# Four tiles instead of two for the decoded words of layer 2's weights, and the plain block's weight sums four steps later

## The chip, the cores and the metric

The kernel runs on one core of a Trainium2 chip. The metric is device time in microseconds (us) for one execution; times are given as the median of several runs. The five engines are TensorE (PE; its weight loads appear as PEld), VectorE (DVE), ScalarE (ACT), GpSimd (POOL) and SyncE (SP). SP issues nearly all DMA transfers here, from one queue that is worked through in order.

## What is computed

Three layers over 6016 tokens (2 batches of 3008) of 256 channels, all in float32 with weights that arrive as 64-bit words:

```python
def _attn_ref(x, filt_r, filt_i):            # a convolution by FFT along the sequence
    Y = np.fft.rfft(x, axis=1) * (filt_r + 1j * filt_i)[None, :, :]
    return np.fft.irfft(Y, n=x.shape[1], axis=1)
def _moe_ref(x, w_gate, w_val, w_out):       # layer 1: 256 -> 1536 -> 256
    g = x @ w_gate
    return (g * (1.0 / (1.0 + np.exp(-g))) * (x @ w_val) @ w_out)
def _moe2_ref(x, w_in, w_out):               # layer 2: 256 -> 2048 -> 256
    h = x @ w_in
    return h * np.clip(h + 3.0, 0.0, 6.0) / 6.0 @ w_out
```

## The kernel before

**Stages.** First comes the FFT stage (matrix products with small cosine and sine matrices), to about 70 us. Then come the six token blocks of layer 1, and after them the six blocks of layer 2. Layer 1's block 0 is the **plain block**; it is cut into two halves of 512 tokens. Blocks 1 to 5 of layer 1 and all blocks of layer 2 are computed in **units**.

**Precision.** Every operand of a product is split into a high and a low part (ACT copies to the high part, DVE or POOL subtracts it to get the low one), and three of the four partial products are summed.

**The plain block** is the loop `for t in range(2 * plain)` at L560, 24 steps t. A step computes gate and value of one chunk f of 128 hidden channels for one half (`l1`, L229), ACT applies Silu (L586), DVE multiplies (L593); in every odd step the hidden values of two chunks are split (L607) and the output products of the step pair before run (`l2_plain`, L237). Beside it the layer 1 weights are decoded, one chunk f at a time, from 64-bit to 32-bit words. The list comprehension at L588 sets when: `lead` (ACT `start`, L183, then DVE parts 0 to 2: L192, L194, L197) at t = 2f-6, `rest` (DVE L200, L202, L119) at t = 2f-5, and `part` (ACT L395 writes the high part into `wall(f)`, POOL the low part, SP stores the words into `w1f[f]`, L400) at t = 2f-4. Chunk f is first used at step 4*(f//2) + f%2, so chunks 10 and 11 in steps 20 and 21.

**Weight sums.** The units use a seven-product scheme for 2x2 blocks of matrices and need four sums of weight quarters for each chunk (`weight_sums`, L241, four POOL operations). For chunks 0 to 4 this happens in the plain block, L616 to L627: SP reloads the words from `w1f[q]` (L523, tile `y`), two steps later POOL forms the sums, one step later SP stores them (L520). Steps 19 to 21 ask for the first three units' weights (`ask_unit`, SP, L497, tile `st`), steps 20 and 22 split them (`split_unit`, L501: three ACT casts at L509, five POOL subtractions, tiles `wu` and `wo`). In steps 19 and 20 `to_time` (L156) brings the next block's tokens from the FFT stage into PSUM.

**A unit s** (loop at L829) takes 21 matmuls of `product` (L654) in seven threes and 12 output matmuls (L699) of the unit before it, in three fours. Unit s also splits the weights of unit s+2 and asks for those of unit s+4. The spots "N", "A", "B", "T", "C" inside a unit run jobs that other code has hung there. Blocks 1 to 5 start at units 0, 12, 24, 36 and 48.

**Decoding layer 2's weights** hangs on blocks 2 to 5, 12 units each: four halves per block, 16 in all. A half loads 512 raw words (`ask_w2`, SP, L178, tile `raw`), ACT takes absolute values into tile `wa` (L183), DVE makes tile `ww` and works back into `wa` (L192, L194, L197, L200, L202), POOL adds the two (L119 through `finish_w2`, L805), and every second half POOL forms sums into tile `sm`. One unit later SP stores `ww` into `w2f[g]` (L800) and `sm` (L802). The pool `late` gives each of `raw`, `wa` and `ww` two tiles, `sm` has one. In the fourth unit of a block (units 15, 27, 39, 51) spot "B" holds, in this order, the POOL adds of the second half, DVE's L192 and L194 of the third half, and ACT's L183 of the fourth half:

```python
free_spots = [(u, name) for u in range(7) for name in "ABC" if (u, name) not in ((0, "B"), (1, "A"))]
...
    places = [(s + u, name) for u, name in free_spots[4 * q:4 * q + 5]]
    add(u - 2, "N", ask_w2, g, i)
    add(u - 1, "B", lambda g, i: dec2[g, i].start(), g, i)
    spread(places, [(decode_w2, g, i, 0, 1), (decode_w2, g, i, 2), (decode_w2, g, i, 3), (decode_w2, g, i, 4), (finish_w2, g, i)])
```

In the same unit, behind the L119 `gv` sum, PE's third group of two products ends in DVE's L119 `h<-gv,h` (the value `v1`), which reads the PSUM bank that PE's next product (S4) adds to.

Of the kernel before, what the change touches and what calls it, by code (L numbers as in the profile page):

```python
# [9 lines left out]
F32 = mybir.dt.float32  # L10
# [6 lines left out]
P = 128  # L17
# [6 lines left out]
F1, F2 = DFF1 // P, DFF2 // P  # L24
# [54 lines left out]
def fft_conv_glu_mlp(ctx: ExitStack, tc: tile.TileContext, x, filt, mats, sgn, w1, w2, out):  # L79
# [19 lines left out]
    def wall(f):  # L99
        return wall_a[:, f] if f < 8 else wall_b[:, f - 8]  # L100
# [10 lines left out]
    def bank(tag="gv"):  # L111
        turn[tag] += 1
        return banks[tag][(turn[tag] - 1) % 4]
# [4 lines left out]
    def plus(out, a, b, engine=None):  # L118
        (engine or nc.vector).tensor_tensor(out=out, in0=a, in1=b, op=ALU.add)  # L119
# [28 lines left out]
    def to_time(g, first, n, accs, a, at=0):  # L148

        t0, t1 = turns(first, n)  # L150
        lo, hi = 32 * first, 32 * first + n // 2
        for t in range(t0, t1):
            i0, i1 = max(lo, t * N1), min(hi, (t + 1) * N1)
            for o in range(0, P, 64):
                for r in range(2):
                    nc.tensor.matmul(accs[r][o:o + 64, at + i0 - lo:at + i1 - lo],  # L156
                                     g[rows(r, N1P), t - t0, o:o + 64],
                                     mat[rows(r, N1P), FIN + i0 - t * N1:FIN + i1 - t * N1])
# [7 lines left out]
    class Decode:  # L166
# [17 lines left out]

        def part(self, i, engine=None):
            if self.w is None:
                self.w = self.pool.tile([P, self.n], F32, tag="ww", name="ww")
            v, a, w = nc.vector, self.a, self.w
            au, wu, low, high = a.bitcast(U32), w.bitcast(U32), self.raw[:, :, 0], self.raw[:, :, 1]

            if i == 0:
                v.tensor_scalar(out=a, in0=a, scalar1=LEAST, scalar2=MOST, op0=ALU.max, op1=ALU.min)  # L192
            elif i == 1:
                v.tensor_scalar(out=wu, in0=au, scalar1=3, scalar2=0x3FFFFFF8,  # L194
                                op0=ALU.logical_shift_left, op1=ALU.bitwise_and)
            elif i == 2:
                v.scalar_tensor_tensor(out=wu, in0=high, scalar=0xC0000000, in1=wu,  # L197
                                       op0=ALU.bitwise_and, op1=ALU.bitwise_or)
            elif i == 3:
                v.tensor_scalar(out=au, in0=wu, scalar1=0xFF800000, scalar2=None, op0=ALU.bitwise_and)  # L200
            elif i == 4:
                v.scalar_tensor_tensor(out=a, in0=low, scalar=2.0 ** -52, in1=a, op0=ALU.mult, op1=ALU.mult)  # L202
            else:
                plus(w, w, a, engine or nc.gpsimd)
# [16 lines left out]
    def half(k):  # L221
        return blocks[k][2] * N2 // 2

    def l1(acc, w, c, xs, part=(0, 1, 2)):

        for i in part:
            r, v = ((0, 0), (0, 1), (1, 0))[i]
            for k in range(2):
                nc.tensor.matmul(acc, w[:, r, c[k]:c[k] + P], xs[:, v, k],  # L229
                                 start=(r, v, k) == (0, 0, 0), stop=(r, k) == (1, 1))  # L230

    def l2_plain(k, p, hs, first, last):
        for v, ws in ((0, (1, 0)), (1, (0,))):
            for j in range(2):
                for i in range(2):
                    for r in ws:
                        yield lambda v=v, j=j, i=i, r=r: nc.tensor.matmul(  # L237
                            banks["a"][2 * j + k], wall(2 * p + i)[:, r, (1 + j) * P:(2 + j) * P], hs[:, v, i],
                            start=first and (v, i, r) == (0, 0, 1), stop=last and (v, i) == (1, 1))
# [8 lines left out]
    def new_hs():  # L248
        return mlp.tile([P, 4096], F32R, tag="hs", name="hs")

    def new_h():
        return mlp.tile([P, 2048], F32, tag="h", name="h")
# [10 lines left out]
    with tc.manual_schedule():  # L263
# [130 lines left out]
        def high_w1(f):  # L394
            nc.scalar.copy(out=wall(f)[:, 0], in_=dec[f].w)  # L395
# [44 lines left out]
        def form(j):  # L440
            if j == 0:
                xsd["both"] = new_xs()
            xsd[j] = xsd["both"][:, j * 2048:(j + 1) * 2048].rearrange("p (v k n) -> p v k n", v=2, k=2)
            accs = [bank("a"), bank("a")]
            for a in range(2):
                to_time(gt[j][a], FIRST[j][0], 512, accs, a, 256 * a)
            return accs

        def form_end(j, acc):
            for r in range(2):  # L450
                split(*time_halves(xsd[j], acc, r))
# [108 lines left out]
        for t in range(2 * plain):  # L560
            p, i = divmod(t, 2)
            k, g_ = steps[p]
            f = 2 * g_ + i
            if t == 2 * plain - 5:
                scope.close()
                lower.close()
                for name in ("stage", "raw"):
                    pool[name] = ctx.enter_context(tc.tile_pool(name=name, bufs=1))

            if i == 0:  # L570
                hid[p] = new_h().rearrange("p (a n) -> p a n", n=512)
            gate, val = bank(), bank()
            for part in ((0, 1), (2,)):
                l1(gate, wall(f), (3 * P, 4 * P), xsd[k], part)
                l1(val, wall(f), (0, 5 * P), xsd[k], part)
            if t == 0:
                acc1 = form(1)
            if t in (19, 20):
                turned_x = [bank(), bank()]
                to_time(g1[t - 19], *blocks[1][1:2], 2 * half(1), turned_x, t - 19)  # L580
            if i == 1 and p >= 1:
                kq, gq = steps[p - 1]
                for step in l2_plain(kq, gq, hid.pop(p - 1), gq == 0, gq == G1 - 1):
                    step()
            h = hid[p][:, i]
            nc.scalar.activation(out=h, in_=gate, func=AF.Silu)  # L586

            lead, rest, part = ([f_ for f_ in range(2, F1) if t == 2 * f_ + d] for d in (-6, -5, -4))  # L588
            for f_ in part:
                high_w1(f_)  # L590
            for f_ in lead:
                dec[f_].start()
            nc.vector.tensor_tensor(out=h, in0=h, in1=val, op=ALU.mult)  # L593
            if t == 0:
                form_end(1, acc1)
            for f_ in part:
                low_w1(f_, nc.gpsimd)
                if f_ + 2 < F1:
                    load_dec(f_ + 2)
            for f_ in rest:  # L600
                dec[f_].rest(nc.vector)
            for f_ in lead:
                dec[f_].part(0)
                dec[f_].part(1)
            if i == 1:
                hs = new_hs()[:, :2048].rearrange("p (v a n) -> p v a n", v=2, a=2)
                split(hs[:, 0], hs[:, 1], hid[p][:, 0:2])  # L607
                hid[p] = hs
            for f_ in lead:
                dec[f_].part(2)  # L610
            if t in (8, 10, 12, 14):
                store(1, 1, t - 8)
                store(1, 1, t - 7)
            if t == 9:
                g1 = load_g(*blocks[1][:2], 2 * half(1))
            if 6 < t < 19:  # L616
                q, r = divmod(t - 7, 2)
                if r == 0:
                    if q == 0:
                        spare = new_y()  # L620
                        wq = load_wq(0, spare[:, :768])
                    else:
                        sums(q - 1, wq, spare[:, 1536:].rearrange("p (s c) -> p s c", c=P), nc.gpsimd)
                        if q < 5:
                            wq = load_wq(q, spare[:, 768 * (q % 2):768 * (q % 2) + 768])
                elif q > 0:
                    keep_sums(q - 1)  # L627
            if t in (19, 20, 21):
                ask_unit(t - 19)
            if t in (20, 22):  # L630
                split_unit((t - 20) // 2)
            if t in (19, 20):
                if t == 19:
                    xr[1] = new_raw()
                    begin_x(1)
                evacuate(1, turned_x, t - 19)
            if t > 19:
                for i in ((0,), (1, 2), (3,), ())[t - 20]:
                    differ(1, i)
                for i in ((0, 3), (5, 4, 1), (2, 6), ())[t - 20]:  # L640
                    x_high(1, i)
                for i in ((0,), (3, 5), (4, 1), (2, 6))[t - 20]:
                    x_low(1, i)
# [172 lines left out]
        for k in range(2, n_block):  # L816
            s = F1 * (k - 1)
            for q in range(4):
                g, i = divmod(4 * (k - 2) + q, 2)
                places = [(s + u, name) for u, name in free_spots[4 * q:4 * q + 5]]  # L820
                u, name = places[0]
# [145 lines left out]
```

## Time and profile before

| | |
|---|---|
| median of 3 runs | 1200.11 us (1197.69 to 1200.96) |
| the profiled execution | 1203.46 us, its span 1201.7 us |
| PE busy | 1130.1 us, 94% of the span |
| DVE busy | 852.8 us, 71% |
| ACT busy | 752.6 us, 63% |
| POOL busy | 595.3 us, 50% |
| mean granted TensorE clock | 0.967 of full speed |

A busy share is a mean over stages. Busy time on PE includes time at the lower clock (1.2 instead of 2.4 GHz), where the same matmul takes twice as long. In the rows below, an arrow names what ended an idle time; "x4" counts instructions merged into one row.

### The profile page before, as it was taken

The page shows a single profiled execution, that of the slowest core. Times are in us where ns is not written, and L with a number is a line of the kernel's source. Part 1 is how long each engine was busy: PE and PEld are TensorE (multiplying, and loading weights), DVE is VectorE, ACT ScalarE, POOL GpSimd, SP SyncE. Part 2 cuts the span into 40 slices and gives each one's busy share as a digit, 9 for nine tenths or more (in the row PEclk, how much of TensorE's full clock was granted, in tenths as well). Part 3 has the DMA queues.
Part 4 walks back from the last instruction along what each step waited for, and adds up shares of the span by engine and source line. Part 5 has one row for each costly group of instructions (what it writes and reads, how often), then busy time and mean ns, then how long its engine had stood idle before and what let it go on. Part 6 is the DMA issues. An engine that isn't in the chain of part 4 may idle for free. (4 is left out here: it accounts for less than half of the span.)

```text
span 1201.7 us, 19167 instructions
## 1 busy us (share of the span) xinstructions
PE 1130.1 (94%) x7232; PEld 934.0 (78%) x7232; DVE 852.8 (71%) x1164; ACT 752.6 (63%) x1363; POOL 595.3 (50%) x779
## 2 busy tenths in 40 slices
PE   9989999999599869968996999999999999999998
PEld 7768878888488748846885888888888888888887
DVE  4979966678378756846784887767767767677665
ACT  4644437677267636744773777777777677777664
POOL 4733446746375635555454764544544445335440
PEclk9989989999799979988997999999999999999999
DMA  9965943732633352362324333232232322322300
GB/s 304 282 179 178 281 149 108 201 125 95 172 98 105 127 127 84 106 160 98 108 99 171 108 133 105 73 139 73 73 143 73 124 89 73 140 73 73 108 25 33
DMA packets 59484, 150.65 MB, mean 125 GB/s; under 512 B 5536, under 2 KB 27424, under 8 KB 57888
## 3 DMA queue, kind: packets, MB, share of 16 engines
q1 hardware_dynamic: 58848, 148.92, 38.7%
q8 instruction: 56, 0.92, 0.3%
q10 hardware_dynamic: 544, 0.52, 0.1%
q14 instruction: 36, 0.29, 0.1%
HBM read 117.17 MB, written 32.24 MB: 124 GB/s over the span
## 5 line engine op out<-in xcount | busy, mean ns | idle before, releaser
L654 PE MATMUL gv<-xs,wu 128*128 128x512 f32 (+1 forms) x2268 | 577.6, 391 | 56.6 <-DVE h L119 55.8
L116 POOL TENSOR_TENSOR wu<-st,wu 128x224 fp32r<-128x224 f32 x432 | 308.3, 744 | 489.4 <-ACT wu L509 476.4
L654 PEld LDWEIGHTS gv<-xs,wu 128*128 128x128 f32 x2268 | 427.5, 190 | 145.0 <-DVE h L119 59.3
L699 PE MATMUL a<-hs,wo 128*128 128x512 f32 (+1 forms) x1872 | 479.9, 387 | 0.0
L699 PEld LDWEIGHTS a<-hs,wo 128*128 128x128 f32 x1872 | 353.2, 189 | 67.5 <-ACT hs L687 0.3
L687 ACT CAST hs<-h 128x512 fp32r<-128x512 f32 (+3 forms) x216 | 172.6, 799 | 176.5 <-DVE h L681 101.3
L116 DVE TENSOR_TENSOR hs<-h,hs 128x1024 fp32r<-128x1024 f32 (+3 forms) x228 | 233.6, 1025 | 65.9 <-ACT hs L687 60.5
L116 POOL TENSOR_TENSOR wo<-st,wo 128x256 fp32r<-128x256 f32 x156 | 147.7, 959 | 0.0
L683 DVE SCALAR_TENSOR_TENSOR h<-h,gv 128x512 f32<-128x512 f32 (+1 forms) x144 | 96.4, 670 | 23.3 <-ACT h L677 23.0
L509 ACT CAST wu<-st 128x384 fp32r<-128x384 f32 x216 | 110.6, 563 | 0.0
L119 DVE TENSOR_TENSOR gv<-gv,h 128x512 f32<-128x512 f32 (+1 forms) x108 | 74.0, 685 | 50.7 <-PE gv L654 45.1
L675 ACT ACTIVATE h<-gv 128x512 f32<-128x512 f32 (+1 forms) x120 | 70.5, 588 | 59.3 <-PE gv L654 58.9
L677 ACT ACTIVATE h<-gv 128x512 f32<-128x512 f32 (+1 forms) x144 | 84.0, 583 | 16.3 <-PE gv L654 16.2
L119 DVE TENSOR_TENSOR h<-gv,h 128x512 f32<-128x512 f32 (+1 forms) x108 | 72.9, 675 | 24.5 <-PE gv L654 24.4
L862 ACT COPY gv<-gv 128x512 f32<-128x512 f32 (+1 forms) x108 | 60.8, 563 | 45.4 <-PE gv L654 41.8
L683 DVE SCALAR_TENSOR_TENSOR h<-h,h 128x512 f32<-128x512 f32 (+1 forms) x48 | 32.7, 681 | 59.6 <-ACT h L677 59.6
L866 ACT COPY h<-gv 128x512 f32<-128x512 f32 (+1 forms) x108 | 62.4, 578 | 18.7 <-PE gv L654 17.9
L681 DVE TENSOR_TENSOR h<-h 128x512 f32<-128x512 f32 (+1 forms) x60 | 60.1, 1001 | 3.5 <-ACT h L675 3.2
L116 DVE TENSOR_TENSOR xs<-raw,xs 128x512 fp32r<-128x512 f32 (+1 forms) x77 | 56.8, 739 | 0.1
L509 ACT CAST wo<-st 128x256 fp32r<-128x256 f32 (+1 forms) x108 | 54.2, 501 | 0.0
L194 DVE TENSOR_SCALAR ww<-wa 128x512 uint32<-128x512 uint32 x16 | 9.5, 593 | 60.7 <-DMA w2f<-ww 59.9
L552 ACT CAST xs<-raw 128x512 fp32r<-128x512 f32 (+1 forms) x77 | 45.7, 608 | 3.0 <-DVE raw L116 3.0
(88 smaller groups left out, 940.2 us busy)
## 6 DMA issues: line engine op xcount, KB each, us to landing
st<-w1f SPq DMA_DIRECT2D x60, 576.0 KB, 4.1
st<-w2f SPq DMA_DIRECT2D x48, 704.0 KB, 4.0
raw<-w_in SPq DMA_DIRECT2D x16, 512.0 KB, 4.4
ring<-x_in SPq DMA_DIRECT2D x30, 256.0 KB, 5.4
x<-w_in SPq DMA_DIRECT2D x9, 768.0 KB, 5.5
d<-turned SPq DMA_DIRECT2D x32, 192.0 KB, 5.5
w1f<-x SPq DMA_DIRECT2D x12, 384.0 KB, 2.7
yd<-y SPq DMA_DIRECT2D x4, 1024.0 KB, 6.4
```

The costliest lines, as they stand in the source:

```text
L116: (engine or nc.vector).tensor_tensor(out=out, in0=a, in1=b, op=ALU.subtract)
L119: (engine or nc.vector).tensor_tensor(out=out, in0=a, in1=b, op=ALU.add)
L509: nc.scalar.copy(out=to[:, 0, at:at + hi - lo], in_=src[:, lo:hi])
L654: nc.tensor.matmul(acc[:, :n], w[:, r, FORM[a] * P:(FORM[a] + 1) * P], xs_part(k, v, i), start=start and q == 0, stop=q == 2, skip_group_c ...
L675: nc.scalar.activation(out=self.value(t, 0), in_=src, func=AF.Silu)
L677: nc.scalar.activation(out=self.value(t, a), in_=src, func=AF.Relu, bias=3.0)
L681: nc.vector.tensor_tensor(out=self.value(t, 0), in0=self.value(t, 0), in1=src, op=ALU.mult)
L683: nc.vector.scalar_tensor_tensor(out=self.value(t, a), in0=self.value(t, a), scalar=6.0, in1=src, op0=ALU.min, op1=ALU.mult)
L687: nc.scalar.copy(out=self.hs[:, t, :, 0, :self.n], in_=self.value(t))
L699: yield lambda t=t, v=v, a=a, j=j, r=r: nc.tensor.matmul(banks["a"][2 * j + t][:, :n], self.wo[:, r, (2 * a + j) * P:(2 * a + j + 1) * P], ...
L862: nc.scalar.copy(out=b2[:, :n], in_=b1[:, :n])
L866: nc.scalar.copy(out=u.s7, in_=b3[:, :n])
```

## The change

The tag `ww` gets four tiles where the pool's default of two held before. In the plain block, `lead`, `rest` and `part` of chunks 10 and 11 come one step later (`+ (f > 9)`), and the chain that loads, sums and stores the weight sums of chunks 0 to 4 comes four steps later (q counts from step 11, not 7). No instruction is added or removed.

```diff
@@ Decode.part @@
             if self.w is None:
-                self.w = self.pool.tile([P, self.n], F32, tag="ww", name="ww")
+                self.w = self.pool.tile([P, self.n], F32, tag="ww", name="ww", bufs=4)
@@ the plain block @@
-            lead, rest, part = ([f_ for f_ in range(2, F1) if t == 2 * f_ + d] for d in (-6, -5, -4))
+            lead, rest, part = ([f_ for f_ in range(2, F1) if t == 2 * f_ + d + (f_ > 9)] for d in (-6, -5, -4))
...
-            if 6 < t < 19:
-                q, r = divmod(t - 7, 2)
+            if 10 < t < 23:
+                q, r = divmod(t - 11, 2)
```

**On DVE, in unit 15** (names: `wa`, `ww` and `raw` are the decode tiles, `gv` a PSUM bank, the brackets hold the semaphores waited for, DMAHW those of DMA transfers):

```order
 L192 TENSOR_SCALAR wa<-wa 128x512 [waits Pool_49]
-L194 TENSOR_SCALAR ww<-wa 128x512 [waits DMAHW0_49,DVE_49]
+L194 TENSOR_SCALAR ww<-wa 128x512 [waits DVE_49]
 L119 TENSOR_TENSOR h<-gv_110,h 128x480 [waits PE_49]
 L681 TENSOR_TENSOR h<-h,gv_109 128x480 [waits PE_49,Activation_49]
-L197 SCALAR_TENSOR_TENSOR ww<-raw,ww 128x512 [waits DVE_49]
+L197 SCALAR_TENSOR_TENSOR ww<-raw,ww 128x512 [waits DMAHW0_49,DVE_49]
```

The order stays; L194 no longer waits for a DMA transfer, and the wait that L197 shows now is for the transfer that brings `raw`.

**On DVE, in steps 17 to 19 of the plain block** (`x_122` holds the chunk that is decoded, here chunk 11; `gv_109` and `gv_107` are the values of an even and an odd step):

```order
 L197 SCALAR_TENSOR_TENSOR x_122<-x_122 128x768
-L593 TENSOR_TENSOR h<-h,gv_109 128x512
+L593 TENSOR_TENSOR h<-h,gv_107 128x512
 L200 TENSOR_SCALAR x_122<-x_122 128x768
 L202 SCALAR_TENSOR_TENSOR x_122<-x_122 128x768
 L119 TENSOR_TENSOR x_122<-x_122 128x768
-L116 TENSOR_TENSOR hs<-h,hs 128x1024
-L593 TENSOR_TENSOR h<-h,gv_109 128x512
 L593 TENSOR_TENSOR h<-h,gv_107 128x512
 L116 TENSOR_TENSOR hs<-h,hs 128x1024
```

In step 18 the multiplication (L593, `gv_109`) and before it the low part of step 17's hidden values (L116 `hs`) stood behind the three operations that finish chunk 11; now those two stand ahead of the three, and step 19's multiplication (`gv_107`) comes behind them.

**On POOL, at the end of the plain block** (`wall_b` is the low part of a decoded chunk of layer 1, the `y` rows are one chunk's sums, `wu` and `wo` a unit's split):

```order
 L116 TENSOR_TENSOR wall_b<-x_122,wall_b 128x768
-L116 TENSOR_TENSOR wu<-st,wu 128x224 x4
-L116 TENSOR_TENSOR wo<-st,wo 128x256
+L119 TENSOR_TENSOR y<-y 128x128
+L116 TENSOR_TENSOR y<-y 128x128 x3
+L116 TENSOR_TENSOR wu<-st,wu 128x224 x4
+L116 TENSOR_TENSOR wo<-st,wo 128x256
+L119 TENSOR_TENSOR y<-y 128x128
+L116 TENSOR_TENSOR y<-y 128x128 x3
```

and on SP, whose queue runs in this order:

```order
 L523 DMA y<-w1f_91 128x768
-L400 DMA w1f_97<-x_122 128x768
+L497 DMA st<-w1f_87 128x1152
 L520 DMA w1f_90<-y 128x512
-L400 DMA w1f_98<-x_122 128x768
+L497 DMA st<-w1f_88 128x1152
+L497 DMA st<-w1f_89 128x1152
 L520 DMA w1f_91<-y 128x512
```

The sums of chunk 3 now stand ahead of unit 0's split on POOL and those of chunk 4 ahead of unit 1's; on SP the store of chunk 3's sums stands between the requests for units 0 and 1, and that of chunk 4's behind the request for unit 2.

## Rows read from the trace of the kernel before

**Rows 1.** The page, part 2: PE's busy tenths and clock in 40 slices.

```profile
PE   9989999999599869968996999999999999999998
PEclk9989989999799979988997999999999999999999
```

**Rows 2.** Waits, whole span: waiter, releaser: total us, times, longest.

```profile
DVE ww L194 <- DMA w2f<-ww: 59.9, 4, 16.8
...
PE gv L654 <- DVE h L119: 55.8, 4, 15.8
...
ACT wa L183 <- POOL ww L119: 15.9, 4, 4.2
...
PE gv L156 <- DVE h L593: 2.1, 1, 2.1
```

**Rows 3.** Timeline, units 14 to 16: start us, length us, engine, line [idle before].

```profile
301.50 2.14 PE L654 MATMUL gv<-xs,wu 128*128 128x480 f32 x9
...
306.95 2.53 POOL L116 TENSOR_TENSOR wu<-st,wu 128x224 fp32r<-128x224 f32 x4 [3.04 <-issue]
...
307.82 1.03 PE L699 MATMUL a<-hs,wo 128*128 128x480 f32 x4
...
311.56 0.67 ACT L183 ACTIVATE wa<-raw 128x512 f32<-128x512 f32 x1 [3.91 <-POOL ww L119]
...
322.77 0.43 DVE L194 TENSOR_SCALAR ww<-wa 128x512 uint32<-128x512 uint32 x1 [15.93 <-DMA w2f<-ww]
...
323.82 3.97 PE L654 MATMUL gv<-xs,wu 128*128 128x480 f32 x9 [14.97 <-DVE h L119]
324.35 0.59 ACT L687 CAST hs<-h 128x480 fp32r<-128x480 f32 x1 [12.13 <-DVE h L681]
...
327.58 1.28 PE L699 MATMUL a<-hs,wo 128*128 128x480 f32 x4
```

**Rows 4.** DMA issues at 306.00 and 309.76 us: last number us to landing.

```profile
st<-w1f SPq DMA_DIRECT2D x1, 576.0 KB, 8.9
...
w2f<-ww SPq DMA_DIRECT2D x1, 256.0 KB, 12.9
```

**Rows 5.** Window of 1 us: busy PE, PEld, DVE, ACT, POOL, then PE's clock.

```profile
311.00:312.00 1.00, 0.00 (x0) 0.00 (x0) 0.00 (x0) 0.44 (x1) 0.92 (x2) 0.52 0.98 403
```

**Rows 6.** POOL by form, 286 to 307 us: count, busy us, mean ns.

```profile
L116 POOL TENSOR_TENSOR wu<-st,wu 128x224 fp32r<-128x224 f32 x12 | 9.5, 821 | 7.2 <-ACT wu L509 4.1 <-issue 3.0
L116 POOL TENSOR_TENSOR wo<-st,wo 128x256 fp32r<-128x256 f32 x3 | 3.5, 1151 | 0.0
L119 POOL TENSOR_TENSOR ww<-ww,wa 128x256 f32<-128x256 f32 x2 | 2.0, 1040 | 0.0
```

**Rows 7.** Timeline, PE and DVE in the plain block, steps 12 to 22.

```profile
126.81 5.60 PE L229 MATMUL gv<-xs,wall_a 128*128 128x512 f32 x24
...
134.97 5.60 PE L229 MATMUL gv<-xs,wall_a 128*128 128x512 f32 x24
...
152.57 3.80 PE L229 MATMUL gv<-xs,wall_b 128*128 128x512 f32 x16
...
160.96 2.79 PE L156 MATMUL gv<-mat,g 48*64 48x5 f32 x94 [2.10 <-DVE h L593]
...
171.23 1.60 PE L156 MATMUL gv<-mat,g 48*64 48x5 f32 x96
...
178.34 5.60 PE L229 MATMUL gv<-xs,wall_b 128*128 128x512 f32 x24
```

**Rows 8.** Windows of 1 us in step 19, columns as in rows 5.

```profile
161.00:162.00 1.00, 1.00 (x40) 1.00 (x43) 0.50 (x1) 0.46 (x1) 0.98 (x1) 0.50 1.05 287
...
167.00:168.00 1.00, 1.00 (x5) 0.77 (x4) 0.00 (x0) 0.00 (x0) 0.00 (x0) 0.66 1.00 399
```

**Rows 9.** DVE by form, 102 to 134 us.

```profile
L200 DVE TENSOR_SCALAR x<-x 128x768 uint32<-128x768 uint32 x4 | 2.3, 575 | 0.0
```

**Rows 10.** DVE by form, 134 to 162 us.

```profile
L200 DVE TENSOR_SCALAR x<-x 128x768 uint32<-128x768 uint32 x3 | 2.9, 962 | 0.0
```

## The prediction

> **What bounds the kernel now.** I read the page's slices first: PE is busy nearly everywhere, except in single slices between 300 and 660 us, where its clock falls too [rows 1]. So PE sets the time, and what can be won lies in those holes. The list of waits names them: DVE's L194, which writes `ww`, waits four times for the DMA store of an older `ww`, 59.9 us in all, and PE's L654 waits four times for DVE's L119, 55.8 us in all [rows 2]. Four is once per block 2 to 5. The timeline of unit 15 joins the two: PE stops when its output products end at 307.82 + 1.03 = 308.85 us, DVE resumes with L194 at 322.77 us after 15.93 us of waiting, and PE follows at 323.82 us [rows 3]. L194 stands ahead of the L119 that reads PE's PSUM bank, so a decode step that nobody needs yet holds back the product. The store is late because it was issued at 309.76 us, behind large transfers in SP's queue, and took 12.9 us to land [rows 4].
>
> The hole also costs clock: with PE stopped since 308.85 us, the granted clock from 311 to 312 us is 0.52 [rows 5], the lower level of 1.2 GHz. After the restart nine matmuls take 3.97 us where they took 2.14, and the next four 1.28 instead of 1.03 [rows 3], which is 1.83 + 0.25 = 2.1 us more per hole. Together the four holes cost 55.8 + 4 x 2.1 = 64.2 us.
>
> **The four tiles.** With four tiles a decode half writes a `ww` that was last used a whole block before. The wait of L194 goes, 64.2 us with its clock. What is late next stands in the same unit: ACT's L183 needs the `wa` tile of the half before, which POOL's L119 sets free; `wa` keeps its two tiles. It waits four times today, 15.9 us in all [rows 2], under cover of the longer hole, so it costs nothing; with the cover gone, it is exposed. Behind L183 on ACT stands L687, which writes the high part that PE's output products of the next unit read first.
>
> How long that wait becomes: POOL starts unit 15's split at 306.95 us [rows 3] and does four `wu`, one `wo` and two `ww` operations before `wa` is free. With DVE at work beside it those take 0.821, 1.151 and 1.040 us each [rows 6], so 3.28 + 1.15 + 2.08 = 6.5 us, until 313.5. With DVE waiting, POOL let ACT go at 311.56 us [rows 3]. DVE will be busy for the first half of this time and then wait for ACT itself, so I take the middle, 312.5. Then L183 (0.67) and L687 (0.59) [rows 3] make the high part ready at 313.8; by the ends at 312.8 and 314.7. PE, no longer held, runs its nine products in 2.1 us from 308.85 and would want it at 310.95. It waits 2.85 us (1.9 to 3.8). In step 19 of the plain block an idle time of only 2.1 us [rows 7] was followed by a clock of 0.50 [rows 8]. So I add the 2.1 us of lower clock to a wait of 2.85 us, and leave them out at the short end of 1.9 us, for which no row shows a fall. Per block that is 4.95 us, for four blocks 20 us (7.6 to 23.6). The gain from the four tiles is 64.2 - 20 = 44 us (40.6 to 56.6).
>
> The other waits nearby keep a cover. The next stage load lands 8.9 us after 306.00, at 314.9 us [rows 4]; ACT wants it in unit 16's split. POOL's part of unit 15's began at 306.95, and one unit (301.50 to 308.85, 7.35 us) and the 2.85 us wait later it is 317, so 2 us are to spare. If that cover is gone, each microsecond costs four. The raw words, the stores of `ww` and `sm` and the token loads are the same transfers in the same order; nobody waits for the stores soon, since `sm` is written again more than a unit later.
>
> **Chunks 10 and 11 one step later.** In steady state two steps take 134.97 - 126.81 = 8.16 us; from the start of step 18 to that of step 22 it is 178.34 - 152.57 = 25.77 us, where two pairs and two `to_time` of 1.60 us would make 19.5 [rows 7]. Of the 6.3 us lost, 2.1 are PE's wait for DVE's L593 of step 18 [rows 2, 7], and then the clock stands at its lower level from about 161 to 167.7 us [rows 8], which costs half of 6.7 us, 3.35. The change puts this L593 ahead of the three operations that finish chunk 11, of which L200 alone takes 0.58 to 0.96 us [rows 9, 10] and the other two handle as many words; their time covers the 2.1 us. I take 2.1 + 3.35 = 5.4 us as gain, at most 6.3. Step 19's L593 comes behind the three instead, but PE has two groups of work before it wants that bank. Chunk 11 is first used in step 21, two steps after its high and low part are made.
>
> **Sums four steps later.** Loads (SP), sums (POOL) and stores (SP) keep their number and sizes. On SP they leave the stretch with the token loads; the store of chunk 3's sums now stands between the requests for units 0 and 1. On POOL two chunks of sums stand ahead of the first two splits: eight operations on 128 columns, each at most the 1.04 us of the 256-column form [rows 6], 4.2 us per split. Unit 0's split has the two pairs of steps 20 to 23 as cover, more than 16 us, so I cost it at nothing; if the cover failed, 4 us would be lost there, and no gain follows from it alone.
>
> **The sum** against the profiled execution: 1203.46 - 44.2 - 5.4 = 1153.9 us. That execution lies 3.35 us above the median of the runs; so the median becomes **1150.5 us**. Its own range is 1146 to 1158: at one end waits of 1.9 us with the clock lost and 6.3 us from the plain block, at the other waits of 3.8 us and one split late by 4 us.
>
> **Rivals.** (1) PE's remaining wait is short and the clock stays up: POOL is as quick as with DVE waiting, 1.9 us per block and no clock loss. That gives 1200.11 - 56.6 - 5.4 = 1138 us; with the wait fully hidden 1130. For it: DVE does wait for ACT then. Against: L194 and L197 run beside POOL first.
>
> (2) The plain block gives nothing, as the sums now run in steps 17 and 19, beside chunk 11's decoding: 1200.11 - 44.2 = 1156 us, 4 us more if the splits are late too. DVE's L200 took 0.575 us on average from 102 to 134 us and 0.962 with the sums beside it [rows 9, 10], 0.39 us more, so for three chunks I count some 1.2 us of delay, less than the reordering gives.
> The Trainium skill, page "SBUF — State Buffer", section "SBUF: two separate sides", goes further: DVE and GpSimd share a port pair under an exclusive lock, and the second to come is blocked for the other's whole instruction. By that rule the moved sums block chunk 11's operations rather than slow them a little, and the sum would stay at this rival's 1156 us; the trace bears out that the two get in each other's way, not yet by how much here.
>
> (3) The stage loads come late: without the 15 us pause the queue has no time to drain, and ACT's cast in units 16 to 18 waits 3 to 6 us more per block, clock included: 1163 to 1175 us. For it: landings of 8.9 and 12.9 us [rows 4]. Against: the same bytes, issued at the same times up to unit 15.
>
> (4) Slower than before: the same mechanism, further on. The load for unit 18 would have to land so late that the new hole eats all of 44.2 + 5.4 us, 12.4 us per block beyond the 2 us of slack: 14.4 us after 314.9, 23 us after its issue instead of 8.9. From there each microsecond adds four; at 28 us it is 1220 us. Nothing in rows 4 comes near, so this has little chance.
>
> (5) The four tiles move the wait instead of ending it: L197, two operations later, still waits for a transfer, the one that brings `raw`. If that one were as late as the store, the time would stay at 1195 to 1200 us. That load is issued a unit and more ahead, so it hardly can.
>
> **How the numbers follow.** Forecast 0.57, rivals (1) 0.17, (2) 0.14, (3) 0.08, (4) 0.02, (5) 0.02. A measurement of this kernel can tell about 0.3%, 3.6 us, from no change. Faster: 0.57 + 0.17 + 0.14 + 0.08 = 0.96; within 0.3%: 0.02; slower: 0.02. The range goes from 1138, half of rival (1), over the forecast and rival (2) to 1164 us, with the late splits: 0.57 + 0.14 + 0.09 = 0.80.
>
> **What would show it.** Right, if the list of waits has lost DVE's `ww` behind the store; if ACT's L183 still waits four times for POOL, 5 us each; if PE has four waits of 2 to 4 us at the first output products of units 16, 28, 40 and 52, with the clock low behind each; and if step 18 to step 22 takes 20 to 21 us without a wait of `to_time` for L593. Wrong, if PE's waits there are gone or as long as the old ones, if ACT's casts wait for `st`, or if PE waits for the split of unit 0 or 1.

## The result and the profile after

The changed kernel takes **1143.37 us** (median of 6 runs, 1141.59 to 1144.89) where the kernel before took 1200.53 (6 runs on the same chip, 1197.19 to 1203.26): a ratio of 0.9526 [0.9506, 0.9546], 57.2 us less. The forecast was 1150.5 us with a range of 1138 to 1164, so the result lies inside, 7 us below the forecast. The profiled execution took 1143.04 us, its span is 1141.2 us, and the mean granted clock rose from 0.967 to 0.995.

The page's slices of PE and of its clock, which answer to [rows 1]:

```profile
PE   9999999999999999999999999999999999999998
PEclk9999999999999999999999999999999999999999
```

The single slices between 300 and 660 us in which PE paused and its clock fell are gone. The list of waits of the changed kernel (waiter, releaser: total us, times, longest) shows what took their place:

```profile
ACT wa L183 <- POOL ww L119: 18.6, 4, 4.8
...
PE a L699 <- ACT hs L687: 10.4, 4, 2.6
```

DVE's `ww` behind the store (59.9 us) and PE's L654 behind DVE's L119 (55.8 us) of [rows 2] are no longer in it. ACT's L183 still waits four times, 18.6 us now instead of 15.9, and four waits of PE for ACT's L687 are new. The timeline of the changed kernel in unit 15, the place of [rows 3], in order of time:

```profile
296.62 0.43 DVE L194 TENSOR_SCALAR ww<-wa 128x512 uint32<-128x512 uint32 x1
296.71 3.21 POOL L116 TENSOR_TENSOR wu<-st,wu 128x224 fp32r<-128x224 f32 x4 [3.04 <-issue]
...
300.57 1.40 POOL L119 TENSOR_TENSOR ww<-ww,wa 128x256 f32<-128x256 f32 x2
...
302.00 0.66 ACT L183 ACTIVATE wa<-raw 128x512 f32<-128x512 f32 x1 [4.61 <-POOL ww L119]
302.57 0.57 ACT L687 CAST hs<-h 128x480 fp32r<-128x480 f32 x1
...
303.19 1.97 PE L699 MATMUL a<-hs,wo 128*128 128x480 f32 x4 [2.64 <-ACT hs L687]
```

L194 now runs without a wait. POOL's split and its two adds to `ww` end at 301.97 us, ACT's L183 starts 0.03 us later, L687 follows behind it, and PE follows L687. Before, PE stood still here for 14.97 us.

In the plain block (timeline of PE in the changed kernel) no wait is left from step 18 to step 22:

```profile
147.61 5.60 PE L229 MATMUL gv<-xs,wall_b 128*128 128x512 f32 x24
153.14 1.64 PE L156 MATMUL gv<-mat,g 48*64 48x5 f32 x96
...
160.42 1.61 PE L156 MATMUL gv<-mat,g 48*64 48x5 f32 x96
...
167.53 5.60 PE L229 MATMUL gv<-xs,wall_b 128*128 128x512 f32 x24
```

From step 18 to step 22 it takes 167.53 - 147.61 = 19.92 us; before it was 25.77 [rows 7]. Unit 0 then begins with a wait of PE for DVE's L593 of 0.75 us, where it was 0.25 before.

**Where the time went.** I cut each profiled execution at the same four instructions: PE's first L229 of step 4, and ACT's first L862 of units 0, 12 and 60 (L863 in e9_one_store, whose file is one line longer). The times are in us, from one execution of each kernel. The last two columns are the median of the runs, and the ratio with its 95% interval to runs of the kernel before that were taken beside them (their medians were 1198.93 to 1200.53 us). The expectations below call the first cut step 8; it is step 4's.

| kernel | start to step 4 | step 4 to unit 0 | units 0 to 12 | units 12 to 60 | rest | median | ratio |
|---|---|---|---|---|---|---|---|
| before | 94.17 | 93.76 | 93.12 | 431.06 | 489.59 | 1200.53 | |
| after | 90.49 | 87.13 | 93.20 | 380.86 | 489.52 | 1143.37 | 0.9526 [0.9506, 0.9546] |
| e1_tiles | 89.74 | 93.39 | 93.17 | 383.34 | 489.56 | 1151.87 | 0.9593 [0.9566, 0.9619] |
| e2_plain | 94.81 | 87.17 | 93.19 | 429.66 | 489.57 | 1194.91 | 0.9959 [0.9944, 0.9973] |
| e3_wa3 | 92.49 | 87.14 | 93.17 | 368.18 | 489.52 | 1132.31 | 0.9436 [0.9413, 0.9458] |
| e4_start | 90.62 | 86.99 | 93.14 | 365.17 | 489.48 | 1126.54 | 0.9392 [0.9367, 0.9417] |
| e5_ww3 | 92.31 | 86.92 | 93.12 | 381.97 | 489.58 | 1144.88 | 0.9546 [0.9522, 0.9570] |
| e6_sums_only | 92.05 | 87.40 | 93.16 | 379.22 | 489.57 | 1143.06 | 0.9539 [0.9509, 0.9569] |
| e7_chunks_only | 92.49 | 91.29 | 93.15 | 378.96 | 489.51 | 1146.48 | 0.9557 [0.9536, 0.9579] |
| e8_store_act | 89.93 | 87.06 | 93.15 | 390.09 | 489.47 | 1152.12 | 0.9605 [0.9571, 0.9638] |
| e9_one_store | 93.99 | 88.36 | 93.12 | 382.11 | 489.62 | 1148.87 | 0.9575 [0.9546, 0.9603] |
| e10_put_late | 92.94 | 87.63 | 93.16 | 365.46 | 489.61 | 1130.26 | 0.9426 [0.9408, 0.9443] |

Between before and after, blocks 2 to 5 (units 12 to 60) give 50.2 us and the plain block gives 6.6, together 56.8 us. The stretch before step 4, in which the change touches nothing, varies from 89.7 to 94.8 us between these executions for reasons I did not settle; so the 3.7 us between these two executions there say nothing of the change. Of the stretch from step 4 to unit 0, seven executions have the same code (after, e2, e3, e4, e5, e8, e10); they take 86.92 to 87.63 us, so differences under 0.7 us there mean nothing.

### The profile page after: what moved, and what is told of

Its sections match the earlier page's. It is cut to its first block, busy times and chain, and to the rows that moved or that the text cites. A ratio compares the mean times of both kernels' runs of the same rounds, so it can differ in the third digit from the quotient of the medians.

```text
span 1141.2 us, 19170 instructions
## 1 busy us (share of the span) xinstructions
PE 1119.2 (98%) x7232; PEld 926.9 (81%) x7232; DVE 853.5 (75%) x1164; ACT 752.1 (66%) x1363; POOL 598.0 (52%) x779
## 4 chain that ended last, share of the span: by engine, by line
PE 89%; DVE 3%; issue 2%; POOL 2%; DMA 2%; ACT 1%; SPq 1%; DVEq 0%
PE gv L654 42%; PE a L699 35%; PE gv L229 5%; PE a L237 2%; PE gv L370 1%; PE gv L156 1%; PE gv L328 1%; PE a L344 1%; POOL wu L116 1%; DMA ring<-x_in 1%; DVE h L681 1%; POOL ww L119 0%; DVE xs L116 0%; DMA w1f<-x 0%; DMA d<-turned 0%
## 5 line engine op out<-in xcount | busy, mean ns | idle before, releaser
L654 PE MATMUL gv<-xs,wu 128*128 128x512 f32 (+1 forms) x2268 | 572.2, 388 | 1.2 <-DVE h L593 0.8
L116 POOL TENSOR_TENSOR wu<-st,wu 128x224 fp32r<-128x224 f32 x432 | 311.6, 753 | 423.7 <-ACT wu L509 411.1
L654 PEld LDWEIGHTS gv<-xs,wu 128*128 128x128 f32 x2268 | 424.7, 189 | 87.7 <-DVE gv L119 3.4
L699 PE MATMUL a<-hs,wo 128*128 128x512 f32 (+1 forms) x1872 | 480.6, 387 | 10.4 <-ACT hs L687 10.4
L699 PEld LDWEIGHTS a<-hs,wo 128*128 128x128 f32 x1872 | 352.1, 188 | 79.1 <-ACT hs L687 12.6
L116 DVE TENSOR_TENSOR hs<-h,hs 128x1024 fp32r<-128x1024 f32 (+3 forms) x228 | 234.9, 1030 | 81.0 <-ACT hs L687 75.7
L687 ACT CAST hs<-h 128x512 fp32r<-128x512 f32 (+3 forms) x216 | 172.5, 799 | 132.2 <-DVE h L683 73.9
L116 POOL TENSOR_TENSOR wo<-st,wo 128x256 fp32r<-128x256 f32 x156 | 147.7, 959 | 0.0
L675 ACT ACTIVATE h<-gv 128x512 f32<-128x512 f32 (+1 forms) x120 | 70.6, 588 | 57.1 <-PE gv L654 56.8
L119 DVE TENSOR_TENSOR gv<-gv,h 128x512 f32<-128x512 f32 (+1 forms) x108 | 73.9, 685 | 43.7 <-PE gv L654 38.1
L119 DVE TENSOR_TENSOR h<-gv,h 128x512 f32<-128x512 f32 (+1 forms) x108 | 72.9, 675 | 25.7 <-PE gv L654 25.4
L862 ACT COPY gv<-gv 128x512 f32<-128x512 f32 (+1 forms) x108 | 60.9, 564 | 42.7 <-PE gv L654 39.1
L116 DVE TENSOR_TENSOR xs<-raw,xs 128x512 fp32r<-128x512 f32 (+1 forms) x77 | 56.8, 739 | 0.1
L229 PE MATMUL gv<-xs,wall_a 128*128 128x512 f32 x192 | 45.4, 391 | 0.0
```

The lines of the kernel that those rows point to most:

```text
L229: nc.tensor.matmul(acc, w[:, r, c[k]:c[k] + P], xs[:, v, k], start=(r, v, k) == (0, 0, 0), stop=(r, k) == (1, 1))
L654: nc.tensor.matmul(acc[:, :n], w[:, r, FORM[a] * P:(FORM[a] + 1) * P], xs_part(k, v, i), start=start and q == 0, stop=q == 2, skip_group_c ...
L675: nc.scalar.activation(out=self.value(t, 0), in_=src, func=AF.Silu)
L687: nc.scalar.copy(out=self.hs[:, t, :, 0, :self.n], in_=self.value(t))
L699: yield lambda t=t, v=v, a=a, j=j, r=r: nc.tensor.matmul(banks["a"][2 * j + t][:, :n], self.wo[:, r, (2 * a + j) * P:(2 * a + j + 1) * P], ...
```

## The experiments

**The two parts apart.** e1_tiles keeps the four `ww` tiles and undoes the plain block's part; e2_plain does the opposite.

```diff
e1_tiles, against the changed kernel
-            lead, rest, part = ([f_ for f_ in range(2, F1) if t == 2 * f_ + d + (f_ > 9)] for d in (-6, -5, -4))
+            lead, rest, part = ([f_ for f_ in range(2, F1) if t == 2 * f_ + d] for d in (-6, -5, -4))
...
-            if 10 < t < 23:
-                q, r = divmod(t - 11, 2)
+            if 6 < t < 19:
+                q, r = divmod(t - 7, 2)
e2_plain, against the changed kernel
-                self.w = self.pool.tile([P, self.n], F32, tag="ww", name="ww", bufs=4)
+                self.w = self.pool.tile([P, self.n], F32, tag="ww", name="ww")
```

> Only the four tiles, the plain block as before. Theory (each part works by itself, the holes of blocks 2 to 5 belong to the tiles): the units keep their gain of about 50 us, the plain block its loss of about 7 us between steps 14 and 22, so about 1150 us, and PE's wait of 2.1 us for DVE's L593 in step 19 is back. Rival (the two parts need each other, as the splits of the first units and the sums share POOL): more than 1156 us.

> Only the plain block's shift, ww with two tiles. Theory: four waits of DVE's L194 for the store of ww, 15 us each, and four holes on PE as before; only the 6 to 7 us of the plain block are gained, so about 1193 to 1195 us. Rival (the shift alone does nothing, and what the profile of the changed kernel shows between steps 14 and 22 differs from one execution to the next): 1198 to 1201 us.

e1_tiles took 1151.87 us, e2_plain 1194.91, against 1143.37 with both. Against the kernel before (1200.53 us, and 1198.93 in the runs beside these two) the tiles are thus worth 47 to 49 us alone and the plain block 4 to 6; behind the tiles the plain block is worth 8.5. The cuts say where: e1_tiles has the long plain block (93.39) with short blocks (383.34), e2_plain the short plain block (87.17) with long blocks (429.66). Between the profiled executions of e1_tiles and the changed kernel, 6.3 us stand in the plain block and 2.5 in units 12 to 60, where the code is the same and the clock of e1_tiles fell once more (last section). In e2_plain's list of waits the two large waits of [rows 2] stand as they were:

```profile
DVE ww L194 <- DMA w2f<-ww: 59.0, 4, 16.4
...
PE gv L654 <- DVE h L119: 55.0, 4, 15.4
```

**The wait that is left.** The forecast said that ACT's L183, waiting for POOL to free a `wa` tile, would now hold back L687. Two ways to take that away: a third `wa` tile, so that L183 need not wait for POOL; or L183 of the block's fourth half one spot later, so that L687 no longer stands behind it.

```diff
e3_wa3, against the changed kernel
-                self.a = self.pool.tile([P, self.n], F32, tag="wa", name="wa")
+                self.a = self.pool.tile([P, self.n], F32, tag="wa", name="wa", bufs=3)
e4_start, against the changed kernel
-                add(u - 1, "B", lambda g, i: dec2[g, i].start(), g, i)
+                add(*((u, "A") if q == 3 else (u - 1, "B")), lambda g, i: dec2[g, i].start(), g, i)
```

> The changed kernel, and three tiles for wa. Theory (PE's four remaining waits of 2.6 us are ACT's wait in L183 for the wa tile that POOL still reads): they go, with the low clock behind them, 10 us of idle time and 2 to 4 us of clock, so about 1130 us. Rival (POOL or the stage loads end last right behind, and take the wait over): 1138 us or more.

> The changed kernel with two wa tiles, but the fourth half's L183 stands half a unit later on ACT, in spot A of the next unit. Theory (the wait costs because L183 stands ahead of L687 in ACT's queue, not because POOL is late with the tile): the same as three tiles, about 1130 us, and L183 waits for nothing or under 1 us. Rival (POOL's end itself is what the unit needs): no gain, 1141 us or more.

Both remove the four waits of PE, and both beat the changed kernel: 1132.31 and **1126.54 us**, the best of all here (0.9392 [0.9367, 0.9417] of before). In e4_start's timeline the L687 in question runs at 298.46 us, well ahead of L183 at 302.98, and PE's output products at 300.32 have no bracket behind them, so they did not wait:

```profile
298.46 0.60 ACT L687 CAST hs<-h 128x480 fp32r<-128x480 f32 x1 [1.13 <-DVE h L681]
...
300.32 1.03 PE L699 MATMUL a<-hs,wo 128*128 128x480 f32 x4
...
300.92 2.03 POOL L119 TENSOR_TENSOR ww<-ww,wa 128x256 f32<-128x256 f32 x2
...
302.98 0.68 ACT L183 ACTIVATE wa<-raw 128x512 f32<-128x512 f32 x1 [0.88 <-POOL ww L119]
```

POOL is no earlier than in the changed kernel (its two adds end at 302.95 us, there at 301.97), and L183 still waits four times for POOL, 3.5 us in all; only the order in ACT's queue has changed. That is the cost, shown: not POOL's time but what stands behind the waiting L183. In e3_wa3's list of waits, L183 waits for its other input instead, the raw words, and its blocks take 0.75 us each longer than e4_start's ((368.18 - 365.17) / 4):

```profile
ACT wa L183 <- DMA raw<-w_in: 6.3, 4, 1.6
```

**How many tiles, and why the store is late.** e5_ww3 gives `ww` three tiles instead of four. e8_store_act goes back to two tiles and lets ACT issue the store of `ww`, so that it no longer stands in SP's queue.

```diff
e5_ww3, against the changed kernel
-                self.w = self.pool.tile([P, self.n], F32, tag="ww", name="ww", bufs=4)
+                self.w = self.pool.tile([P, self.n], F32, tag="ww", name="ww", bufs=3)
e8_store_act, against e2_plain
-                nc.sync.dma_start(out=w2f[g][:, 512 * i:512 * i + 512 - P * i], in_=w[:, :512 - P * i])
+                nc.scalar.dma_start(out=w2f[g][:, 512 * i:512 * i + 512 - P * i], in_=w[:, :512 - P * i])
```

> The changed kernel with three tiles for ww. Theory (only the third half's wait for the store of the first mattered, and what waits now is one half later): L194 of the fourth half comes some 14 us after the third's and waits about 2 us for a store that lands 13 us after its issue, so four short waits on DVE, and 1144 to 1152 us. Rival (every reuse within a block costs a hole of its own): 1160 us or more.

> Two ww tiles, with the plain block's shift, and the stores of ww issued from ACT's queue instead of SP's. Theory (the store is late because it stands behind raw, token and stage loads in SP's queue): it is issued about 4 us sooner and passes them, L194 waits 2 to 5 us instead of 15, and the time is 1145 to 1165 us. Rival (the DMA engines are simply busy then, whichever queue asks): the waits stay above 10 us each, 1185 us or more.

e5_ww3 took 1144.88 us, not to be told from the 1143.37 of four tiles. Its list of waits still has L194 behind the store, but the waits are short, and PE's waits are nearly those of four tiles (10.9 us for ACT's L687 against 10.4):

```profile
DVE ww L194 <- DMA w2f<-ww: 6.9, 3, 3.0
```

e8_store_act took 1152.12 us, 42.8 of the 51.5 us that four tiles give over e2_plain, with the two old tiles. The timeline has the store on ACT's queue at 293.56 us, ahead of SP's load of `raw`, and the third half's L194 without a wait behind it; the DMA view gives 2.0 us from issue to landing, where SP's queue took 12.9 us [rows 4]:

```profile
293.56 0.35 ACTq L800 DMA_DIRECT2D w2f<-ww  x1
294.19 0.33 SPq L178 DMA_DIRECT2D raw<-w_in  x1
...
295.97 0.43 DVE L194 TENSOR_SCALAR ww<-wa 128x512 uint32<-128x512 uint32 x1
...
313.60 0.43 DVE L194 TENSOR_SCALAR ww<-wa 128x512 uint32<-128x512 uint32 x1 [5.21 <-DMA w2f<-ww]
```

```profile
w2f<-ww ACTq DMA_DIRECT2D x1, 256.0 KB, 2.0
...
w2f<-ww ACTq DMA_DIRECT2D x1, 192.0 KB, 8.9
```

So it was the place behind SP's loads that made that store late: here it goes out 0.63 us ahead of the load of `raw`, in the kernel before 4.66 us behind it (305.10 and 309.76 us). That ACT's queue lets a store pass loads that are already under way is not shown. The last row of each view speaks against it: the next store, issued at 304.19 us while those loads were under way (the stage loads among them took 12.4 us to land), took 8.9 us on ACT's queue too, and the fourth half's L194 waited 5.21 us for it. There the rival held (the DMA engines are busy, whichever queue asks). These waits are longer than the 2 to 5 us expected, and through DVE's L116, which stands behind L194, they reach PE:

```profile
DVE ww L194 <- DMA w2f<-ww: 15.2, 3, 6.1
...
PE a L699 <- DVE hs L116: 6.4, 3, 3.1
```

Units 12 to 60 of e8_store_act are 9.2 us longer than those of the changed kernel (390.09 against 380.86); 6.4 of them are these waits, and the rest was not followed.

**Which half of the plain block's change pays.** Both have four `ww` tiles. e6_sums_only moves the weight sums and leaves chunks 10 and 11 at their old steps; e7_chunks_only does the reverse.

```diff
e6_sums_only, against the changed kernel
-            lead, rest, part = ([f_ for f_ in range(2, F1) if t == 2 * f_ + d + (f_ > 9)] for d in (-6, -5, -4))
+            lead, rest, part = ([f_ for f_ in range(2, F1) if t == 2 * f_ + d] for d in (-6, -5, -4))
e7_chunks_only, against the changed kernel
-            if 10 < t < 23:
-                q, r = divmod(t - 11, 2)
+            if 6 < t < 19:
+                q, r = divmod(t - 7, 2)
```

> The changed kernel with chunks 10 and 11 at their old steps; only the sums come four steps later. Theory (the wait of to_time for DVE's L593 is the order of chunk 11's operations on DVE): step 8 to unit 0 takes about 92 us in the trace, against 87.1 changed and 93.8 before, and the whole about 1148 us. Rival (the sums beside the decoding made DVE late): about 87 to 88 us in that stretch, 1144 us.

> The changed kernel with the sums at their old steps; only chunks 10 and 11 come one step later. Theory (order of chunk 11's operations on DVE): step 8 to unit 0 takes 87 to 88.5 us in the trace, and the whole about 1144 us. Rival (the sums beside the decoding made DVE late): 91 us or more there, 1148 us.

The stretch from step 4 to unit 0 takes 93.39 us with neither (e1_tiles), 91.29 with the chunks moved, 87.40 with the sums moved and 87.13 with both. Moving the sums gives 6.0 us; moving the chunks gives 2.1 alone, and behind the sums 0.3, which is not to be told from nothing. Both expectations had it the other way round: the theory fell and the rival held. In PE's timeline of e6_sums_only the wait of `to_time` for step 18's L593 is small, and the clock behind it stays up (94 matmuls in 1.60 us):

```profile
155.53 1.60 PE L156 MATMUL gv<-mat,g 48*64 48x5 f32 x94 [0.56 <-DVE h L593]
```

In that of e7_chunks_only the wait is there in spite of the new order on DVE, with a second one ahead of it, and the next twelve L237 take 4.60 us instead of 3.06 (the changed kernel's):

```profile
141.84 1.19 PE L237 MATMUL a<-hs,wall_a 128*128 128x512 f32 x4 [1.14 <-DVE hs L116]
...
158.30 1.60 PE L156 MATMUL gv<-mat,g 48*64 48x5 f32 x94 [1.45 <-DVE h L593]
159.83 4.60 PE L237 MATMUL a<-hs,wall_b 128*128 128x512 f32 x12
```

**What the sums did in the old place.** In the kernel before, the list of waits and POOL's timeline show POOL standing in front of its first sum (L119 `y`) until the store of the previous chunk's sums has landed, since all chunks share one result tile; chunk 8's low part (L116 `wall_b`) queues behind:

```profile
POOL y L119 <- DMA w1f<-y: 11.5, 3, 9.4
```

```profile
135.05 0.76 POOL L119 TENSOR_TENSOR y<-y 128x128 f32<-128x128 f32 x1 [9.38 <-DMA w1f<-y]
...
138.07 2.56 POOL L116 TENSOR_TENSOR wall_b<-x,wall_b 128x768 fp32r<-128x768 f32 x1
```

There it meets DVE's last operations on the next chunk (DVE's timeline of the kernel before):

```profile
137.82 1.10 DVE L202 SCALAR_TENSOR_TENSOR x<-x 128x768 f32<-128x768 uint32 x1
138.96 2.49 DVE L119 TENSOR_TENSOR x<-x 128x768 f32<-128x768 f32 x1
```

That L119 takes 0.96 us where POOL does nothing beside it. Here it takes 2.49 and ends at 141.45 us, 0.82 after POOL's operation (140.63); POOL's own took 2.56 us instead of 1.86 to 1.90, and it ended 1.71 after the DVE operation that was running when it began (138.92). Each looks as if it had done its work only once the other was through. The Trainium skill, page "SBUF — State Buffer", section "SBUF: two separate sides", says that DVE and GpSimd share a port pair under an exclusive lock, which one holds for its whole instruction; it names a DVE operation with two SBUF inputs beside a GpSimd one that reads SBUF as such a case. These two rows agree with it: L202 and L119 have two inputs each.

e9_one_store takes the wait away without moving the sums: they are formed in the old steps, but the stores one by one are left out, and in step 18 the last result is stored five times.

```diff
e9_one_store, against e1_tiles
-                elif q > 0:
-                    keep_sums(q - 1)
+                elif q == 5:
+                    for f_ in range(5):
+                        nc.sync.dma_start(out=w1f[f_][:, 6 * P:], in_=formed[4].rearrange("p s c -> p (s c)"))
```

> Four ww tiles, chunks and sums at their old steps, but the sums are not stored one by one: in step 18 the last result is stored five times, so the weights of layer 1's blocks 1 to 5 hold wrong sums for chunks 0 to 3 (the stores of four results are left out, their number and sizes stay). Theory (what made DVE late is POOL's wait of 9 us for the store of the sums before, which pushes the low parts and the sums behind it onto DVE's later operations): step 8 to unit 0 takes 87 to 89 us in the trace instead of 93.4. Rival (the sums themselves, wherever they stand in that stretch, block DVE): 91 us or more.

The stretch falls from 93.39 to 88.36 us, 5.0 of the 6.0 us that moving the sums gave. Here POOL's sums wait for their load once, 4.46 us where the wait for the store was 9.38, and for no store. Chunk 8's low part starts at 132.82 instead of 138.07 us and takes 1.86 us; it meets DVE's L192 now (1.44 us instead of 0.56), and none of the three operations that finish a chunk, so L119 takes 0.96 us (timelines of POOL, DVE and PE):

```profile
129.65 0.96 POOL L119 TENSOR_TENSOR y<-y 128x128 f32<-128x128 f32 x1 [4.46 <-DMA y<-w1f]
...
132.82 1.86 POOL L116 TENSOR_TENSOR wall_b<-x,wall_b 128x768 fp32r<-128x768 f32 x1
...
139.15 0.96 DVE L119 TENSOR_TENSOR x<-x 128x768 f32<-128x768 f32 x1
...
158.45 1.60 PE L156 MATMUL gv<-mat,g 48*64 48x5 f32 x94 [1.53 <-DVE h L593]
159.98 3.01 PE L237 MATMUL a<-hs,wall_b 128*128 128x512 f32 x12
```

A rival, that the traffic of the stores held up the loads of the words to be decoded, finds no support: ACT's L183 waits 1.55 us for the words of chunk 9 here and 1.68 in the kernel before, and for those of chunks 10 and 11 in neither.

Three limits to this. The medians (1148.87 against 1151.87 us for e1_tiles) do not separate the two kernels, their intervals overlap; the evidence is the cut of one execution each. About 1.5 of the 5.0 us are clock: in e1_tiles the 94 and 12 matmuls behind the wait took 1.85 and 4.30 us, here 1.60 and 3.01; and since the clock fell in e7_chunks_only behind a wait of 1.45 us, it may be luck that it stayed up here behind 1.53. And the 1.53 us that remain were not taken apart: with the same order on DVE and the sums four steps later the wait is 0.56 us (e6_sums_only), so the order on DVE is not all of it. In the changed kernel POOL's sums still wait for a store, once, where it holds up no step of PE:

```profile
POOL y L119 <- DMA w1f<-y: 4.6, 1, 4.6
```

**A miss.** In e4_start, PE waits nowhere in blocks 2 to 5 for more than 0.4 us, but ACT's cast of the stage loads waits five times for `st`. e10_put_late moves the store of a finished block's tokens four units later, out of the way of those loads.

```profile
ACT wu L509 <- DMA st<-w1f: 6.3, 5, 2.0
```

```diff
e10_put_late, against e4_start
-                add(now[0] + 2, "N", put_y, k, ys[k])
+                add(now[0] + 6, "N", put_y, k, ys[k])
```

> The half unit later L183 of e4_start, and the store of a finished block's tokens four units later, so that 1 MB less stands ahead of the stage load of unit 18. Theory (what ends last now is this stage load: ACT's cast waits 6.3 us for st in all): the casts wait under 1 us each, blocks 2 to 5 lose another 0.7 us each, so about 1124 us. Rival (the token loads behind it are as large and hold the next stage load instead): 1126 us as before.

ACT's waits for `st` shrank from 6.3 to 1.0 us, and units 12 to 60 stayed at 365.46 us (365.17 in e4_start). The theory that the loads still hold these blocks fell. The median, 1130.26 us, is no better than e4_start's 1126.54; the profiled executions differ only in the stretches ahead of unit 0 (92.94 and 87.63 against 90.62 and 86.99), and why is open.

## Why the prediction was right, and where it was wrong

**L194's wait and its clock: right.** The holes were put at 64.2 us. e4_start has no hole, and its units 12 to 60 are 431.06 - 365.17 = 65.9 us shorter than before.

**L183 exposed: right in kind and place, a little too dear.** The four waits were put at 2.85 us each, 1.9 to 3.8; they are 10.4 us in all, 2.6 each. With the clock they were put at 20 us, and cost 380.86 - 365.17 = 15.7, if e4_start is taken as free of them. So the wait itself was 1.0 us less than the sum of the forecast, and what is left for the clock behind it is 5.3 us instead of 8.4. The step that was too high is "I add the 2.1 us of lower clock to a wait of 2.85 us" for all four. PE's rows behind the wait in block 2 (the four L699 at 303.19 us, above, and these) put the loss at (1.97 - 1.04) + (2.09 - 1.46) = 1.6 us:

```profile
304.96 2.09 PE L654 MATMUL gv<-xs,wu 128*128 128x480 f32 x6
306.89 1.04 PE L699 MATMUL a<-hs,wo 128*128 128x480 f32 x4
307.77 1.46 PE L654 MATMUL gv<-xs,wu 128*128 128x480 f32 x6
```

In blocks 3 and 4 it is 1.6 and 1.7 us in the same way, in block 5 it is 0.2, together 5.1. So the clock was lost in three blocks, and 1.6 to 1.7 us in each. In the windows of 1 us of the changed kernel, block 2's wait of 2.64 us is followed by the lower level, and block 5's wait, of the same 2.64 us, by full speed (columns as in [rows 5]):

```profile
303.00:304.00 1.00, 0.81 (x2) 0.74 (x3) 0.82 (x2) 1.00 (x3) 1.00 (x3) 0.50 1.11 169
306.00:307.00 1.00, 1.00 (x5) 0.83 (x5) 0.53 (x1) 0.00 (x0) 0.00 (x0) 0.85 1.24 191
595.00:596.00 1.00, 1.00 (x6) 0.82 (x5) 1.00 (x2) 0.72 (x3) 0.26 (x1) 1.00 0.94 385
```

So rival (1), which said the clock would stay up, was partly true, in one block of four of this execution. With the same four waits, the clock fell behind all four in e1_tiles (383.34 us for units 12 to 60) and behind two in e6_sums_only and e7_chunks_only (379.22 and 378.96).

**Chunks 10 and 11: right amount, wrong cause.** The plain block was put at 5.4 us and gave 6.6. But the step "their time covers the 2.1 us" credits the order on DVE with the whole wait and the clock behind it, and this step failed: the order alone gives 2.1 us (e7_chunks_only), and PE's wait for L593 remains there, 1.45 us. Most of the delay came from a part of the trace that I had not followed back: POOL, and on it the wait for the store of the previous sums (e9_one_store, with the limits said there).

**Sums four steps later: wrong.** "I cost it at nothing" was right for the new place, where units 0 to 12 take 93.20 us (93.12 before). The words "no gain follows from it alone" were wrong, and they are the step that failed here: 6.0 us follow from it alone (e6_sums_only), and that is nearly all that the plain block gave. Rival (2) had the mechanism, POOL's sums beside the decoding on DVE, in the wrong place: it expected them to start to hurt in steps 17 and 19, where they hurt less than in the old steps. Its forecast for steps 18 to 22, no gain, fell with 19.92 us against 25.77.

**The other rivals.** (3) The stage loads: ACT waits 0.6 us for `st` in the changed kernel, once; with (3) falls (4). (5) The wait did not move to L197; that it can move to the raw words is seen in e3_wa3, 6.3 us in four times.

**The 7 us between forecast and result**: from the plain block 6.6 - 5.4 = 1.2, from the holes before 1.7, from the waits left 1.0 and their clock 3.1. That is 7.0, and the median differs from the forecast by 1150.5 - 1143.4 = 7.1. So close a match is luck: units 12 to 60 alone take from 378.96 to 383.34 us in executions with the same code there.

## What to carry to other kernels

Where a tile's reuse waits for a store, look at what stands behind the waiting instruction in its engine's queue: here PE's loss was set by that order, at the first wait (L194 ahead of L119) and again at the next (L183 ahead of L687), and moving one instruction a spot later gave 15.7 us in these blocks beyond what the tiles gave. Before a gain is credited to a new order on one engine, follow its lateness back through the engines that feed it; the wait of a reused tile for its store that was removed in one stage also sat in the other, unnoticed, on POOL. When a cover goes, price what it hid, with and without the clock.

## What the runs showed of the hardware that was not expected

**Equal waits, unequal clocks.** The same four matmuls after the same wait of 2.64 us in block 5 took 1.14 us in the changed kernel and 1.97 in e1_tiles (the two timelines):

```profile
594.16 1.14 PE L699 MATMUL a<-hs,wo 128*128 128x480 f32 x4 [2.64 <-ACT hs L687]
```

```profile
599.78 1.97 PE L699 MATMUL a<-hs,wo 128*128 128x480 f32 x4 [2.64 <-ACT hs L687]
```

In e1_tiles the granted clock was then 0.50, the lower level, in both of these windows:

```profile
600.00:601.00 1.00, 1.00 (x3) 0.86 (x4) 1.00 (x2) 1.00 (x3) 0.87 (x2) 0.50 0.93 393
605.00:606.00 1.00, 1.00 (x4) 0.79 (x4) 0.00 (x0) 0.98 (x3) 0.76 (x2) 0.50 0.93 344
```

That block took 92.23 us there and 89.89 in the changed kernel. In the plain block a wait of 1.45 us was followed by the lower level (e7_chunks_only), one of 1.53 us by full speed (e9_one_store); the prediction had left the clock out of its short end, 1.9 us, since no row showed a fall there. Which of the two a given wait brings, none of these runs foretells.

**Two queues.** Of two stores on ACT's queue in e8_store_act, the one issued ahead of SP's loads (256 KB) landed after 2.0 us, and the one issued behind them (192 KB) after 8.9 us; on SP's queue, behind the loads, the store of 256 KB took 12.9 us. What these rows show to matter is what was asked for before the store; a gain from the second queue itself is not shown.
